# Streamed weights read back from sixteen parts of one DRAM tile instead of from a contiguous copy each

## The chip, the cores and the metric

The kernel runs on one core of a Trainium2 chip. The metric is the device time of one execution in microseconds; lower is better. Times given as a median come from several unprofiled runs; the profile is of one execution with the hardware profiler on. In what follows PE is the matmul engine (PEld its weight loads), DVE the vector engine, ACT the scalar engine, POOL the general-purpose engine and SP the sync engine, which here does nothing but issue transfers. Sixteen DMA engines carry every transfer, whichever engine issues it. SBUF has 128 rows (partitions).

## The reference

The input x is 2048 rows of 1024 numbers in bf16. Each row is first layer-normalised. Two things are then computed from the normalised rows and added to x. Path A is an attention over 64 segments of 32 rows, one after the other, with a memory of 8 rows that the next segment takes from the output of the one before:

```python
for s in range(n_seg):                       # 64 segments, strictly in order
    h = jnp.concatenate([mem, xs], axis=1)   # 8 memory rows + 32 rows of x
    q = jnp.einsum('btd,dhe->bhte', h, Wq)   # 32 heads of 128; Wk, Wv the same
    ...
    p = _softmax(jnp.where(mask, scores * scale, -1e9))
    o = jnp.einsum('bhte,hed->btd', jnp.einsum('bhqk,bhke->bhqe', p, v), Wo)
    mem = o[:, :M, :].copy()
    outs.append(o[:, M:, :])
```

Path B picks the two rows with the highest router score, sends them through a gated feed-forward block (w_gate, w_up, w_down) and adds the result to those rows.

## The kernel before

**Weights.** Wq, Wk, Wv and Wo are 32 MB together, more than SBUF holds. They are cut into 64 granules of 128 x 2048 numbers (512 KB): granules 0 to 47 are eight granules (one for each 128 rows of the model dimension) for each of six phases (q, k and v, each in two halves of the heads), granules 48 to 63 are two heads of Wo each. 44 granules stay in SBUF, three are kept in pieces, and seventeen are read anew in every segment; they are listed in `streamed`. Three of the seventeen (11, 15 and 58) have some of their columns kept on chip, so that 1600, 1536 and 1728 columns of each row travel instead of 2048.

**The copies.** In the inputs a row of such a granule is part of a longer row. In segment 0 each streamed granule is therefore copied, from DRAM to DRAM, into a tile of its own (`wsc[g]`, 128 rows one behind the other). `copy_block` issues the copies on POOL's queue, in three batches of at most six, among the work of segment 0 that prepares the memory rows of all segments (the "left rows"). Segments 1 to 63 read these tiles.

**The stream.** `fetch` takes the next granule of the list `flow`, gets one of five slots (`wstream`, each 128 rows of 4 KB) and issues its load on SP's queue. `after` calls it when PE has been given the last matmul of a streamed granule, so the next load waits for that slot alone. The order is that of the program; nothing is planned at run time. A streamed granule is used by PE in the loop over phases (line 862) or in `project` (line 922). For the whole of segments 1 to 63 SP issues hardly anything else; POOL issues the small transfers of a segment (the rows of x, the prepared values QKL and VL, the outputs).

**Loads from sixteen places.** Rows of x are also addressed as `x_left = x2.rearrange("(t s r) d -> t s r d", t=4, s=16)`. The left rows of a tile t are `x_left[t, :, XM:SEG, :]`: the last 8 rows of 16 segments, that is sixteen places in DRAM, 64 KB apart, with eight consecutive rows of 2 KB each, for 128 rows of SBUF. They are loaded at the start (tile XLR, line 230, two loads on SP's queue and two on ACT's) and once more at the end (tile XLS, line 683, four loads on SP's queue). VL, a small tile of prepared values, is read from sixteen places too (line 619). All other large loads name 128 rows on both sides, but for four loads of w_down at the end (line 503), which reach 64 rows of SBUF each.

Of the kernel before, what the change touches and what calls it, by code (L numbers as in the profile page):

```python
# [8 lines left out]
BF16 = mybir.dt.bfloat16  # L9
# [13 lines left out]
PART, AT_HOME = 58, 320  # L23
# [9 lines left out]
def kernel(  # L33
# [16 lines left out]
    nc = tc.nc  # L50
    P = 128
    Bsz, S, D = A_x.shape
# [28 lines left out]
    streamed = [1, 4, 11, 15, 21, 23, 29, 34, 37, 41, 45, 47, 50, 54, 56, 58, 63]  # L81
# [4 lines left out]
    def granule_dram(g):  # L86
        if g < 48:
            p, kc = divmod(g, KC)
            mat, half = PHASES[p]
            return Wqkv[mat][kc * P:(kc + 1) * P, 2048 * half:2048 * (half + 1)]  # L90
        w = g - 48
        return Wo2[2 * w * P:(2 * w + 2) * P, :].rearrange("(hh e) d -> e hh d", hh=2)
# [11 lines left out]
    def granule_out(t, g):  # L104
        return t[:, :] if g < 48 else t.rearrange("p (hh d) -> p hh d", hh=2)
# [3 lines left out]
    dram = ctx.enter_context(tc.tile_pool(name="dram", bufs=1, space=DRAM))  # L109
# [12 lines left out]
    ol_d = [dram.tile([P, 16, XL * H], BF16, name=f"ol_d{t}") for t in range(4)]  # L122

    at_home = {PART: AT_HOME, LAST_KEPT: LAST_COLS, GUEST: 512}
    wsc = {g: dram.tile([P, 2048 - at_home.get(g, 0)], BF16, name=f"wsc{g}") for g in streamed}
    r_d = dram.tile([1, S], BF16, name="r_d")

    res_tiles = {}
# [4 lines left out]
    def room(g, name):  # L133
        if g not in place:
            return home(g, [P, 2048], BF16, name)[:, :]
        tag, i = place[g]
        return areas[tag][:, i, :]
# [14 lines left out]
    def travelling(g):  # L152
        w = granule_dram(g)
        if g in (LAST_KEPT, GUEST):
            return [(slice(0, 2048 - at_home[g]), w[:, 0:2048 - at_home[g]])]
        if g != PART:
            return [(slice(0, 2048), w)]
        return [(slice(0, D - AT_HOME), w[:, 0, AT_HOME:D]), (slice(D - AT_HOME, 2048 - AT_HOME), w[:, 1, :])]
# [47 lines left out]
    for s in range(4):  # L206
        nc.vector.tensor_copy(out=SELM[:, s, 0:XM, :],
                              in_=IDENT[:, 32 * s:32 * s + XM].unsqueeze(2).to_broadcast([P, XM, 4]))
# [197 lines left out]
    def fetch():  # L406
        if not flow:
            return
        s, g = flow.pop(0)
        t = wstream.tile([P, 2048], BF16, tag="g", name="g")  # L410
        if g == PART and s < NSEG - 1:
            n = 2048 - AT_HOME
            for c, w in travelling(g) if s == 0 else [(slice(0, n), wsc[g][:, :])]:
                nc.sync.dma_start(out=t[:, c], in_=w)
            t = (OP, t)
        elif s == 0 or g == PART:
            nc.sync.dma_start(out=granule_out(t, g), in_=granule_dram(g))
        elif g in (LAST_KEPT, GUEST):
            nc.sync.dma_start(out=t[:, 0:2048 - at_home[g]], in_=wsc[g][:, :])
            if g == GUEST:  # L420
                t = [t[:, 512 * c:512 * (c + 1)] for c in range(3)]
        else:
            nc.sync.dma_start(out=t[:, :], in_=wsc[g][:, :])
        queued.append((g, t))

    def part(t, jq):
# [45 lines left out]

    def copy_block(g):
        for c, w in travelling(g):
            nc.gpsimd.dma_start(out=wsc[g][:, c] if g in at_home else granule_out(wsc[g], g), in_=w)

    to_copy = list(streamed)
    flow += [(s, g) for s in range(NSEG) for g in (streamed if s else first_streamed) if s or g != GUEST]
# [44 lines left out]
    for g in range(KC):  # L523
        if g in first_streamed:
            assert flow.pop(0) == (0, g)
            t = wstream.tile([P, 2048], BF16, tag="g", name="g")
            queued.append((g, t))
        else:
            t = res_tiles[g] = room(g, f"wres{g}")
# [10 lines left out]
    for g in range(KC, 32):  # L540
        if g == GUEST:
            t = res_tiles[g] = room(v_homes[8], "guest")
            nc.sync.dma_start(out=t, in_=granule_dram(g))
        elif g in first_streamed:
            if len(queued) < N_SLOT:
                fetch()
        else:
            load_resident(g)
        if g >= 8 and g < 15:
            load_x(g - 7)  # L550
# [70 lines left out]
    def left_done(p):  # L621
        for g in range(8 * p, 8 * (p + 1)):
            if g in first_streamed and g != GUEST:
                fetch()
        if p == 0:
            sd_rows(MV[:, 1:NT, :], VE[:, 1:NT])
            spread(1, NT)
            router_tiles()
        elif p == 1:
            res_tiles.pop(GUEST)  # L630
            load_resident(v_homes[8])
            area("big0", [P, 8, 2048], "W8A")
            for g in AREAS["big0"]:
                load_resident(g)
        elif p == 2:
            router_top()
            route_rows()
        elif p == 3:
            route_turns(*routed[0])
            load_resident(hx)  # L640
            home_first()
        elif p == 4:
            area("big1", [P, 8, 2048], "W8B")
        elif p == 5:
            load_resident(hm)
        if p in (1, 2):
            copy_blocks(6)

    def copy_blocks(n):
        for _ in range(min(n, len(to_copy))):  # L650
            copy_block(to_copy.pop(0))

    def after(s, g):

        if g in streamed:
            fetch()
        if s == NSEG - 1:
            if g in resident and g < 48 and g not in place and g not in resident[:3]:
                free_homes.append(g)
            if g in (54, 55):  # L660
                for t in (2 * g - 108, 2 * g - 107):
                    load_left_x(t)
            if g >= 57:
                fetch_moe(1)
# [62 lines left out]
    for s in range(NSEG):  # L727
# [120 lines left out]
        for p, (mat, half) in enumerate(PHASES):  # L848
            PSm = psA.tile([P, 512], F32, tag="acc", name="PSm")
            behind = []  # L850
            for kc in range(KC):
                g = 8 * p + kc
# [3 lines left out]
                for jq in range(4):  # L856
                    rhs = [(0, 512, part(Gv, jq))]
                    if s > 0 and g == LAST_KEPT and jq == 3:
                        n = 512 - LAST_COLS
                        rhs = [(0, n, Gv[:, 1536:1536 + n]), (n, 512, back[g][:, 0:LAST_COLS])]  # L860
                    for c0, c1, w in rhs:
                        nc.tensor.matmul(PSm[32 * jq:32 * jq + 32, c0:c1], lhsT=ST[:, kc, :], rhs=w,  # L862
                                         start=(kc == 0), stop=(kc == KC - 1), tile_position=(0, 32 * jq))
# [250 lines left out]
```

## Time and profile before

| | |
|---|---|
| median of 3 runs | 1817.13 us (1808.01 to 1818.28) |
| the profiled execution | 1815.76 us, span of its instructions 1814.0 us |
| PE busy | 1564.0 us, 86% of the span |
| DVE, ACT, POOL busy | 941.3, 781.4, 331.0 us |
| DMA | 657.62 MB, mean 363 GB/s |
| SP's queue (q1) | 601.13 MB, 88.1% of the time of 16 DMA engines |
| mean granted clock of PE | 0.987 |

The span falls into three stages: up to about 230 us the weights come in and segment 0 runs, with the preparation of the left rows; from 230 to 1725 us segments 1 to 63 run, all alike, some 24 us each; then the left rows' outputs and path B follow. A busy time is the sum over an engine's instructions and says nothing about what it waits for; that stands in the views of waits. The DMA share is the time that packets took on the sixteen engines, and can pass 1 by a few hundredths where a packet's record overlaps the next. Instructions that only issue a transfer are not counted as busy; a view of one tile shows how long each took and how long the transfer was under way.

### The profile page before, as it was taken

Reading aid. Unit: us, or ns where it says so; the run is one execution under the profiler, and the core shown is the slowest. Engines: PE = TensorE matmul, PEld = TensorE weight load, DVE = VectorE, ACT = ScalarE, POOL = GpSimd, SP = SyncE. Lnnn points to the kernel's source line nnn. Section 1 sums busy time; section 2 is a strip of 40 time slices with the busy share of each in tenths; the row PEclk is TensorE's granted clock in tenths of the full one; section 3 lists DMA queues with packets and bytes.
Section 4 is the critical chain, followed back from the end, with each engine's and each line's share of the span. In section 5 each row is a group of like instructions: output and inputs, shape, how many; then the busy total and the mean of one; then the engine's idle time right before and its main releaser. Section 6 shows DMA issues by size and latency. Waiting matters only on the chain. (4 is left out here: it accounts for less than half of the span.)

```text
span 1814.0 us, 70576 instructions
## 1 busy us (share of the span) xinstructions
PE 1564.0 (86%) x30354; PEld 851.3 (47%) x30354; DVE 941.3 (52%) x3027; ACT 781.4 (43%) x2032; POOL 331.0 (18%) x610
## 2 busy tenths in 40 slices
PE   8999888888888888888888888888888888888888
PEld 5444444444444444444444444444444444444455
DVE  6722155555555555555555555555555555555531
ACT  2333144444444444444444444444444444444410
POOL 1021311111111111111111111111111111111220
PEclk9999989999999999999999999999999999999989
DMA  9685899999999999999999999999999999999998
GB/s 359 232 297 192 270 357 368 382 369 375 376 392 386 376 377 379 375 374 375 382 373 387 383 384 366 389 393 370 368 382 383 379 382 369 381 376 378 386 375 300
DMA packets 215833, 657.62 MB, mean 363 GB/s; under 512 B 42800, under 2 KB 46432, under 8 KB 215520
## 3 DMA queue, kind: packets, MB, share of 16 engines
q1 hardware_dynamic: 189232, 601.13, 88.1%
q0 software_dynamic: 25264, 50.14, 8.1%
q8 instruction: 237, 3.88, 0.9%
q10 hardware_dynamic: 1024, 1.84, 0.3%
q14 instruction: 76, 0.62, 0.1%
HBM read 632.01 MB, written 29.56 MB: 365 GB/s over the span
## 5 line engine op out<-in xcount | busy, mean ns | idle before, releaser
L862 PE MATMUL PSm<-wres,ST 128*32 128x512 bf16 x6400 | 501.6, 383 | 0.0
L862 PEld LDWEIGHTS <-ST 128*32 128x32 bf16 x12351 | 325.3, 96 | 351.0 <-issue 111.4
L862 PE MATMUL PSm<-g,ST 128*32 128x512 bf16 (+1 forms) x3017 | 307.0, 380 | 55.9 <-DMA g<-wsc 52.5
L922 PEld LDWEIGHTS <-OT 128*32 128x32 bf16 x8255 | 215.6, 97 | 80.1 <-issue 63.3
L450 ACT COPY BK<-KEPT 128x512 bf16<-128x512 bf16 x252 | 152.3, 605 | 131.2 <-PE WO L922 68.1
L871 ACT CAST XB<-PSm 128x512 bf16<-128x512 f32 x256 | 150.3, 587 | 126.3 <-PE PSm L862 124.8
L668 POOL DMA_DIRECT2D QKL<-ql_d x63 | 46.4, 736 | 773.6 <-ACT OTL L821 756.8
L922 PE MATMUL WO<-W8B,OT 128*32 128x256 bf16 x4096 | 185.6, 276 | 0.2 <-issue 0.2
L862 PE MATMUL PSm<-W8A,ST 128*32 128x512 bf16 x2048 | 182.7, 381 | 0.2 <-DVE RXT L346 0.2
L922 PE MATMUL WO<-g,OT 128*32 128x256 bf16 (+1 forms) x2497 | 130.1, 276 | 46.8 <-DMA g<-wsc 38.4
L450 DVE COPY BK<-KEPT 128x512 bf16<-128x512 bf16 x252 | 106.9, 424 | 121.9 <-ACT BK L450 73.6
L955 POOL DMA_DIRECT2D out_dram<-XN x256 | 131.1, 517 | 177.6 <-DVE XN L951 165.3
L862 PE MATMUL PSm<-BK,ST 128*32 128x512 bf16 x693 | 123.3, 386 | 22.5 <-DVE ST L399 22.5
L892 ACT CAST VM<-PSm 128x512 bf16<-128x512 f32 x128 | 79.7, 623 | 98.3 <-PE PSm L862 98.2
L748 DVE COPY KT<-PSm 128x512 bf16<-128x512 bf16 x126 | 51.0, 405 | 124.3 <-PE PSm L738 124.3
L738 PEld LDWEIGHTS <-XB 128*128 128x128 bf16 x1024 | 58.0, 98 | 105.0 <-ACT XB L871 98.7
L765 DVE TENSOR_TENSOR BS<-BS,CT 128x96 f32<-128x96 f32 (+1 forms) x256 | 59.6, 233 | 90.2 <-PE BS L758 85.7
L738 PE MATMUL PSm<-IDENT,XB 128*128 128x128 bf16 x1008 | 100.5, 222 | 2.8
L743 ACT COPY QT<-PSm 128x512 bf16<-128x512 bf16 x126 | 73.8, 586 | 55.7 <-PE PSm L738 55.7
L783 DVE TENSOR_REDUCE DN<-BS 128x8 f32<-128x320 f32 x128 | 62.8, 490 | 64.4 <-ACT BS L775 64.4
L565 PE MATMUL PSG<-XLT,wres 128*128 128x512 bf16 x336 | 94.4, 383 | 1.1 <-ACT GA L567 0.9
L951 DVE CAST XN<-WO 128x256 bf16<-128x256 f32 x64 | 27.2, 424 | 129.0 <-PE WO L922 129.0
(222 smaller groups left out, 2422.6 us busy)
## 6 DMA issues: line engine op xcount, KB each, us to landing
g<-wsc SPq DMA_DIRECT2D x882, 512.0 KB, 6.1
g<-wsc SPq DMA_DIRECT2D x62, 432.0 KB, 5.7
g<-wsc SPq DMA_DIRECT2D x63, 400.0 KB, 6.1
g<-wsc SPq DMA_DIRECT2D x63, 384.0 KB, 6.4
ql_d<-GA POOLq DMA_DIRECT2D x16, 512.0 KB, 6.6
QKL<-ql_d POOLq DMA_DIRECT2D x63, 128.0 KB, 6.1
MW<-in_B_w_gate_dram SPq DMA_DIRECT2D x16, 448.0 KB, 13.7
wres<-in_A_Wk_dram SPq DMA_DIRECT2D x12, 512.0 KB, 10.2
```

Source lines behind the costliest of these rows:

```text
L450: copy(out=back[g][c], in_=KEPT_COLS[g][c])
L565: nc.tensor.matmul(PSG[:, :], lhsT=part(Gs[kc], h // 4)[:, P * (h % 4):P * (h % 4 + 1)], rhs=XLT[:, :, kc, :], start=(kc == 0), stop=(kc = ...
L738: nc.tensor.transpose(out=PTq[:, il, :, :].rearrange("p j r -> p (j r)"), in_=XB[:, il * P:(il + 1) * P], identity=IDENT[:, :])
L743: nc.scalar.copy(out=QT[half][:, :, :], in_=pv)
L748: (nc.vector.tensor_copy if s else nc.scalar.copy)(out=KT[half][:, :, 0:32], in_=pv)
L765: nc.vector.tensor_tensor(out=S4, in0=S4, in1=m, op=ALU.add)
L783: nc.vector.tensor_reduce(out=DN[:, :], in_=S8, axis=AX.X, op=ALU.add)
L862: nc.tensor.matmul(PSm[32 * jq:32 * jq + 32, c0:c1], lhsT=ST[:, kc, :], rhs=w, start=(kc == 0), stop=(kc == KC - 1), tile_position=(0, 32 ...
L871: nc.scalar.copy(out=XB[:, :], in_=PSm[:, :])
L892: nc.scalar.copy(out=VM[half][:, :], in_=PSm[:, :])
L922: nc.tensor.matmul(PS[32 * g:32 * g + 32, c0:c1], lhsT=lhs(h), rhs=rhs, start=False, stop=(last and hs == 1), tile_position=(0, 32 * g), s ...
L955: nc.gpsimd.dma_start(out=out2[s * SEG:s * SEG + XM, 256 * g:256 * (g + 1)], in_=OB[32 * g:32 * g + XM, :])
```

## The change

The seventeen tiles become one, `wsc_d`, of sixteen parts. Part e holds, for each streamed granule in turn, the eight rows 8e to 8e+7 of the granule, one behind the other, and the next granule's eight rows follow directly. `wsc[g]` is now a view of that tile with sixteen parts of eight runs (`e i c`). A whole granule is thus sixteen pieces of 32 KB, and a part is 33,536 x 8 numbers long. Loads and copies use the view in place of a 128-row tile. Copies of the granules of Wo, which were one transfer with both heads, are issued as one transfer per head. Sizes, slots, queues and the order of loads are untouched.

```diff
     at_home = {PART: AT_HOME, LAST_KEPT: LAST_COLS, GUEST: 512}
-    wsc = {g: dram.tile([P, 2048 - at_home.get(g, 0)], BF16, name=f"wsc{g}") for g in streamed}
+    row_of = {g: 2048 - at_home.get(g, 0) for g in streamed}
+    wsc_d = dram.tile([16, sum(row_of.values()) * 8], BF16, name="wsc_d")
+    wsc, start = {}, 0
+    for g, n in row_of.items():
+        wsc[g] = wsc_d[:, start:start + 8 * n].rearrange("e (i c) -> e i c", i=8)
+        start += 8 * n
...
-            for c, w in travelling(g) if s == 0 else [(slice(0, n), wsc[g][:, :])]:
+            for c, w in travelling(g) if s == 0 else [(slice(0, n), wsc[g])]:
                 nc.sync.dma_start(out=t[:, c], in_=w)
...
-            nc.sync.dma_start(out=t[:, 0:2048 - at_home[g]], in_=wsc[g][:, :])
+            nc.sync.dma_start(out=t[:, 0:2048 - at_home[g]], in_=wsc[g])
...
-            nc.sync.dma_start(out=t[:, :], in_=wsc[g][:, :])
+            nc.sync.dma_start(out=t[:, :], in_=wsc[g])
...
     def copy_block(g):
         for c, w in travelling(g):
-            nc.gpsimd.dma_start(out=wsc[g][:, c] if g in at_home else granule_out(wsc[g], g), in_=w)
+            if g < 48 or g == PART:
+                nc.gpsimd.dma_start(out=wsc[g][:, :, c], in_=w)
+            else:
+                for hh in range(2):
+                    nc.gpsimd.dma_start(out=wsc[g][:, :, D * hh:D * (hh + 1)], in_=w[:, hh, :])
```

## The prediction

> **What bounds the kernel now.** I read the page's slices first, then the waits of the matmul engine, then the queue that issues the streamed loads, then stretches of time side by side. The page's DMA row has each slice's busy share of the sixteen DMA engines in tenths:
>
> ```profile
> DMA  9685899999999999999999999999999999999998
> ```
>
> From the sixth slice to the last but one it stands at 9. That is the stage in which segments 1 to 63 run, from 230 to 1725 us. Its row in the view by stretches (length, busy time and count of each engine, granted clock, DMA share, GB/s):
>
> ```profile
> 230.00:1725.00 1495.00, 1275.71 (x28193) 696.30 (x28190) 826.76 (x2757) 702.37 (x1879) 280.00 (x506) 0.99 1.01 378
> ```
>
> The DMA engines are busy all the time, at 378 GB/s, so the stage moves 1495 us x 378 GB/s = 565 MB. PE is busy for 1276 of the 1495 us. The streamed granules are nearly all of these bytes:
>
> ```profile
> g<-wsc SPq DMA_DIRECT2D x882, 512.0 KB, 6.1
> g<-wsc SPq DMA_DIRECT2D x62, 432.0 KB, 5.7
> g<-wsc SPq DMA_DIRECT2D x63, 400.0 KB, 6.1
> g<-wsc SPq DMA_DIRECT2D x63, 384.0 KB, 6.4
> ```
>
> Counts times sizes give 527,760 KB, 540 MB, in 1070 loads: one load per 1495/1070 = 1.40 us, while one takes 6.1 us from issue to landing. So more than four of the five slots are always under way, and any loss of rate goes straight into the time. PE waits for these loads for 52.5 + 38.4 = 91 us in all (total, times, longest):
>
> ```profile
> PE PSm L862 <- DMA g<-wsc: 52.5, 102, 1.9
> PE WO L922 <- DMA g<-wsc: 38.4, 100, 1.1
> ```
>
> The stage is therefore close to balance: a faster DMA could win at most those 91 us, since PE has work for the rest, but a slower DMA has nothing that hides it.
>
> **What the change does to a load.** No byte and no wait on PE is added. What changes is the form of the 1070 loads: 128 rows on both sides before, 128 rows of SBUF against sixteen parts of eight runs in DRAM now. The kernel before has this form already, in three small places: the tiles XLR (start), XLS (end) and VL are loaded from sixteen places of eight rows each. Here is SP's queue around the turn from one segment of the stage to the next, before (wsc_105 to wsc_121 are the copies of the seventeen granules, g a slot of the stream):
>
> ```order
> L414 DMA g<-wsc_120 128x1728
> L423 DMA g<-wsc_121 128x2048
> L423 DMA g<-wsc_105 128x2048
> L423 DMA g<-wsc_106 128x2048
> L419 DMA g<-wsc_107 128x1600
> ```
>
> and the same place now:
>
> ```order
> L428 DMA g<-wsc_d 128x1x2048 x11
> L419 DMA g<-wsc_d 128x1x1728
> L428 DMA g<-wsc_d 128x1x2048 x3
> L424 DMA g<-wsc_d 128x1x1600
> L424 DMA g<-wsc_d 128x1x1536
> ```
>
> To compare, the first rows of SP's queue, which are the same before and now but for their line numbers:
>
> ```order
> L1118 UNCONDITIONAL_BRANCH
> L235 DMA XLR<-in_A_x_dram 128x1x1024 x2
> L528 DMA g<-in_A_Wq_dram 128x1024
> L528 DMA wres_165<-in_A_Wq_dram 128x1024
> L528 DMA g<-in_A_Wq_dram 128x1024
> ```
>
> Nothing moved in the order, and the first loads of segment 1 still wait for their copies; the loads now have XLR's shape (128x1xn against sixteen by eight) instead of that of the weight loads (128xn). So XLR and XLS are the price list, and there are two prices in it.
>
> *The issue.* Instructions of SP's queue (ns: min/median/max):
>
> ```profile
> L423 SPq DMA_DIRECT2D g<-wsc x882: 319/320/1075, 224.4 to 1725.2; - x177
> L230 SPq DMA_DIRECT2D XLR<-in_A_x_dram x2: 573/640/707, 0.9 to 1.7; - x2
> L683 SPq DMA_DIRECT2D XLS<-in_A_x_dram x4: 604/657/1584, 1725.6 to 1728.6; - x4
> L619 SPq DMA_DIRECT2D VL<-vl_d x2: 533/540/547, 171.2 to 202.1; - x2
> ```
>
> An issue grows from 0.320 to between 0.540 and 0.657 us, by at most 0.337 us. Seventeen of them take 11 us of a segment of 1495/63 = 23.7 us, so the queue keeps up; behind the issuing instruction stands only the next streamed load. I cost it at nothing, because four loads under way cover it. Without that cover each of five slots comes round 0.337 us later: 1070 x 0.337 / 5 = 72 us.
>
> *The rate.* These are stretches of the same run:
>
> ```profile
> 4.00:7.00 3.00, 3.00 (x31) 3.00 (x29) 2.44 (x6) 0.06 (x1) 2.04 (x4) 1.00 1.06 264
> 8.00:12.00 4.00, 2.54 (x36) 1.91 (x33) 2.77 (x6) 1.45 (x3) 0.00 (x0) 1.00 1.06 378
> 1735.00:1738.00 3.00, 2.25 (x12) 0.83 (x12) 0.74 (x3) 0.00 (x0) 0.87 (x2) 0.50 1.05 296
> 1738.00:1741.00 3.00, 3.00 (x8) 1.15 (x7) 2.70 (x5) 0.00 (x0) 3.00 (x7) 0.50 1.06 264
> 1741.00:1750.00 9.00, 9.00 (x43) 5.95 (x42) 6.91 (x23) 2.78 (x3) 2.50 (x5) 0.99 1.03 398
> 1791.00:1798.00 7.00, 7.00 (x34) 4.66 (x33) 0.00 (x0) 0.00 (x0) 0.00 (x0) 1.00 1.07 230
> 1799.00:1803.00 4.00, 4.00 (x64) 2.81 (x56) 2.25 (x8) 0.00 (x0) 0.00 (x0) 1.00 1.05 385
> ```
>
> From 4 to 7 us most of the four XLR loads passes, and the rate is 264 GB/s with the DMA engines busy throughout (share 1.06). At 8 to 12 us half granules pass, in pieces of 2 KB like XLR's, and it is 378. From 1735 to 1741 us the four XLS loads pass: 296 and 264 GB/s, and 398 as soon as they are through. The engines are not idle in the slow stretches; each packet simply takes longer. So the form itself, or where it reads, costs about 30% of the rate. The row at 1791 to 1798 us says where the cost may lie. There the four w_down loads pass that reach only 64 of the 128 SBUF rows, from rows of DRAM that follow each other, at 230 GB/s; the w_down loads of 128 rows behind them run at 385 (1799 to 1803 us). So the way in which a load's rows are dealt out over SBUF can halve the rate by itself. I take it that a load with sixteen parts is dealt out in eights, part by part, so that engines meet on the same piece of SBUF. That is an inference from these rows, not something they show.
>
> [...]
>
> *The copies.* On POOL's queue the four output-projection granules that were one copy each are two now, before (in brackets the counters of POOL's earlier transfers that an issue waits for):
>
> ```order
> L475 DMA wsc_117<-in_A_Wo_dram 256x1x1024 [waits DMASW6_49]
> L475 DMA wsc_118<-in_A_Wo_dram 256x1x1024 [waits DMASW7_49]
> L475 DMA wsc_119<-in_A_Wo_dram 256x1x1024 [waits DMASW0_49]
> L475 DMA wsc_120<-in_A_Wo_dram 128x704 [waits DMASW1_49]
> L475 DMA wsc_120<-in_A_Wo_dram 128x1024
> L475 DMA wsc_121<-in_A_Wo_dram 256x1x1024
> ```
>
> and now:
>
> ```order
> L484 DMA wsc_d<-in_A_Wo_dram 16x8x1024 [waits DMASW6_49]
> L484 DMA wsc_d<-in_A_Wo_dram 16x8x1024 [waits DMASW7_49]
> L484 DMA wsc_d<-in_A_Wo_dram 16x8x1024 [waits DMASW0_49]
> L484 DMA wsc_d<-in_A_Wo_dram 16x8x1024 [waits DMASW1_49]
> L484 DMA wsc_d<-in_A_Wo_dram 16x8x1024 x2
> L481 DMA wsc_d<-in_A_Wo_dram 16x8x704 [waits DMASW4_49]
> L481 DMA wsc_d<-in_A_Wo_dram 16x8x1024 [waits DMASW5_49]
> L484 DMA wsc_d<-in_A_Wo_dram 16x8x1024 [waits DMASW6_49]
> L484 DMA wsc_d<-in_A_Wo_dram 16x8x1024 [waits DMASW7_49]
> ```
>
> Ten copies stand where six stood, so four issues are added, ahead of the GATE copy of the left rows' values. The trace has six such copies and what comes behind them (start, length):
>
> ```profile
> L475 POOL DMA_DIRECT2D wsc<-in_A_Wo_dram x6: 695/944/1152, 133.6 to 136.3; - x6
> 163.81 0.19 POOL L598 COPY CT<-VG 128x4 bf16<-128x4 bf16 x1 [26.37 <-DVE PT L781]
> ```
>
> Four more at 0.944 us are 3.8 us, in front of a gap of 26.37 us in which POOL waits for DVE: nothing on the path. Uncovered it would be 3.8 us.
>
> **The sum.** The profiled execution took 1815.76 us with a span of 1814.0; the median of the runs is 1817.13, 0.1% more. Of the span 319 us lie outside the stage and stay. Inside, 565 MB at the mean of the three rows, (264 + 296 + 264)/3 = 275 GB/s, take 2057 us in place of 1495: +562 us. 1815.76 + 562 = 2378 us. PE's 91 us of waiting are swallowed in that, not added. Bounds for the rate of 4 KB runs, which no row shows in this form: on the bad side the 64-row loads, 230 GB/s, 2457 us of stage, +962 us, and with the uncovered issue +72: 2850 us. On the good side I halve the loss of the mildest row, (296 + 378)/2 = 337 GB/s, 1677 us, +182 us: 1998 us. I take the middle because the three rows are of the very form, and longer runs speak both ways: fewer changes of row, but longer meetings.
>
> **Rivals.**
> 1. *The slow rows are DRAM's doing.* XLR and XLS read 16 KB out of every 64 KB of x, a power of two; the new parts lie 33,536 x 16 = 536,576 bytes apart, 512 KB and 12 KB. If that pitch made the 264 GB/s, the new loads keep 378, the issue is covered, and the time is 1816 us. For it: no load from sixteen parts with another pitch is in the trace at length. Against it: the 64-row loads show the same loss without any pitch. [...]
> 2. *Faster: each engine reads one run of 32 KB per granule, and the next granule's run behind it.* If DRAM rewards that and SBUF does not punish it, PE's waits for the loads go, and PE's own work is next: 1816 - 91 = 1725 us. It decides only if packets get faster than now, and 378 GB/s is already within 5% of the best row above (398). XLR's runs of 16 KB, consecutive as well, show no such reward.
> 3. *Only the issue counts.* The rate stays and the cover is thinner than the median of 6.1 us says: up to 1816 + 72 = 1888 us.
>
> **Chances.** The forecast's case 0.85, rival 1 0.09, rival 2 0.03, rival 3 0.03. The range 2000 to 2850 us holds about 95% of the forecast's case, 0.81 in all. A measurement of this kernel tells about 1% (18 us; its three runs spread over 0.6%) from no change. Slower: 0.85 + 0.03 = 0.88. Within 1%: 0.08, nearly all of rival 1. Faster: 0.04.
>
> **What would show it.** In the changed kernel's stage the DMA share stays at 1.0 while GB/s falls to about 275; packets and bytes of the streaming queue stay as they are and their share of the longer span does not fall. Issue to landing of the loads rises from 6.1 to some 8 or 9 us (the same four loads under way at 1.92 us each), and PE's waits for them grow from 91 to about 600 us; SP's issues read 0.54 to 0.66 us. If GB/s stays at 378 and only the issues are longer, rival 1 holds and the inference on SBUF is wrong. If the stage's rate lies above 337, the form hurts little with runs of 4 KB. If PE's granted clock falls towards 0.50, as in the rows from 1735 to 1741 us, the time goes above my range.

## The result and the profile after

The change made the kernel a third slower: 2420.16 us, median of 6 runs (2413.52 to 2439.69), against 1812.92 us for the kernel before on the same chip (1807.26 to 1818.56). The ratio is 1.3385, with a 95% interval of 1.3338 to 1.3433. The profiled execution took 2438.65 us, its span 2437.0 us. One run behind the times below, of the kernel with two column halves, took 3085.42 us at a granted clock of 0.554 where its others had 0.99, and is left out of their median.

The DMA row of the page (busy share of the DMA engines in tenths, by slices) and the row of the streaming queue (packets, MB, share of the time of sixteen engines) of the changed kernel:

```profile
DMA  9759999999999999999999999999999999999998
...
q1 hardware_dynamic: 189232, 601.13, 92.4%
```

The same row of the kernel before:

```profile
q1 hardware_dynamic: 189232, 601.13, 88.1%
```

The engines are as full as before, and the queue has the same packets and bytes. In the view by stretches, the stage of segments 1 to 63 of the changed kernel (length, busy us and count of PE, PEld, DVE, ACT and POOL, granted clock, DMA share, GB/s):

```profile
230.00:2344.00 2114.00, 1528.24 (x28182) 768.67 (x28181) 831.86 (x2758) 714.42 (x1881) 278.50 (x505) 0.85 1.03 267
```

The stage grew from 1495 to 2114 us, by 619. The other 323 us of the span were 319 before. So all but 4 us of the loss lies in the stage, where 378 GB/s became 267, while the DMA share went from 1.01 to 1.03: the engines were busy all the time before and after. The page's DMA issues (KB each, median us from issue to landing), and the first line of SP's issues in the view of the new tile (ns: min/median/max):

```profile
g<-wsc_d SPq DMA_DIRECT2D x882, 512.0 KB, 9.3
g<-wsc_d SPq DMA_DIRECT2D x62, 432.0 KB, 9.3
g<-wsc_d SPq DMA_DIRECT2D x63, 400.0 KB, 9.2
g<-wsc_d SPq DMA_DIRECT2D x63, 384.0 KB, 9.0
```

```profile
L428 SPq DMA_DIRECT2D g<-wsc_d x882: 514/514/887, 222.6 to 2344.3; - x177
```

A load lands after 9.3 us where it took 6.1, and its issue takes 0.514 us where it took 0.320. What PE waits for, in the view of waits (total us, times, longest), and the first row of the chain that ended last (shares of the span by engine), both of the changed kernel:

```profile
PE PSm L871 <- DMA g<-wsc_d: 343.7, 400, 2.7
PE WO L931 <- DMA g<-wsc_d: 182.6, 238, 2.3
```

```profile
DMA 73%; PE 25%; issue 1%; ACT 1%; DVE 0%; POOL 0%; ACTq 0%; DVEq 0%; SPq 0%
```

The chain is DMA for 73% of the span; that of the kernel before could be followed over only a fifth of its span, so the two can't be compared. PE now waits 526 us for streamed granules instead of 91. It was also busy for longer in the stage, 1528 us instead of 1276, with nearly the same count of matmuls in the trace, at a granted clock of 0.85 instead of 0.99. That did not add to the time: the DMA engines had no idle time to give, and 565 MB at 267 GB/s are 2116 us, which is the stage.

### The profile page after: what moved, and what is told of

It reads as the page before. It is cut to its first block, busy times and chain, and to the rows that moved or that the text cites. A ratio compares the mean times of both kernels' runs of the same rounds, so it can differ in the third digit from the quotient of the medians.

```text
span 2437.0 us, 70581 instructions
## 1 busy us (share of the span) xinstructions
PE 1816.9 (75%) x30354; PEld 923.5 (38%) x30354; DVE 946.3 (39%) x3027; ACT 793.4 (33%) x2032; POOL 331.3 (14%) x614
## 4 chain that ended last, share of the span: by engine, by line
DMA 73%; PE 25%; issue 1%; ACT 1%; DVE 0%; POOL 0%; ACTq 0%; DVEq 0%; SPq 0%
DMA g<-wsc_d 71%; PE PSm L871 11%; PE PSG L574 4%; PE WO L931 3%; PE WD L1005 2%; PE PSV L601 2%; PE PSm L747 1%; DMA vl_d<-VG 1%; PE FIRST L263 0%; DMA wres<-in_A_Wq_dram 0%; DMA out_dram<-XLS 0%; DMA XLR<-in_A_x_dram 0%; PE BS L819 0%; PE PSm L385 0%; DMA wres<-in_A_Wo_dram 0%
## 5 line engine op out<-in xcount | busy, mean ns | idle before, releaser
L871 PEld LDWEIGHTS <-ST 128*32 128x32 bf16 x12351 | 345.5, 103 | 769.6 <-issue 588.2
L871 PE MATMUL PSm<-g,ST 128*32 128x512 bf16 (+1 forms) x3017 | 339.1, 422 | 347.5 <-DMA g<-wsc_d 343.7
L871 PE MATMUL PSm<-wres,ST 128*32 128x512 bf16 x6400 | 571.5, 431 | 0.0
L931 PEld LDWEIGHTS <-OT 128*32 128x32 bf16 x8255 | 256.9, 113 | 281.3 <-issue 238.5
L931 PE MATMUL WO<-g,OT 128*32 128x256 bf16 (+1 forms) x2497 | 161.5, 336 | 191.0 <-DMA g<-wsc_d 182.6
L931 PE MATMUL WO<-W8B,OT 128*32 128x256 bf16 x4096 | 227.0, 326 | 0.0
L871 PE MATMUL PSm<-W8A,ST 128*32 128x512 bf16 x2048 | 195.4, 406 | 0.2 <-DVE CT L353 0.2
L871 PE MATMUL PSm<-BK,ST 128*32 128x512 bf16 x693 | 143.9, 469 | 22.5 <-DVE ST L404 22.5
L828 DVE CAST OT<-BT 128x128 bf16<-128x128 f32 x128 | 37.4, 292 | 212.8 <-PE BT L822 200.8
L828 ACT CAST OT<-BS 128x128 bf16<-128x128 f32 x130 | 34.5, 265 | 233.9 <-PE BT L822 221.2
```

Source lines behind the costliest of these rows:

```text
L828: copy(out=OT[half][:, 2 * ph + jl, :, :], in_=ov[:, :, 0:SEG])
L931: nc.tensor.matmul(PS[32 * g:32 * g + 32, c0:c1], lhsT=lhs(h), rhs=rhs, start=False, stop=(last and hs == 1), tile_position=(0, 32 * g), s ...
```

## The experiments

What was to be settled is why a load of the same bytes has a lower rate. The theory of the prediction (A in the expectations) puts it at the writing into SBUF: engines meet there when the rows are dealt out in eights. Its rivals are DRAM (B, the place of the parts; D, the reading of parts as such) and the issue time (C). For each run I give its time, beside it the kernel before on the same chip, and the stretch from 500 to 1300 us, which lies in the stage of every kernel. In that stretch the kernel before reads:

```profile
500.00:1300.00 800.00, 684.13 (x15182) 374.05 (x15181) 445.46 (x1487) 377.11 (x1013) 147.45 (x266) 1.00 1.01 380
```

and the changed kernel:

```profile
500.00:1300.00 800.00, 576.98 (x10844) 291.84 (x10837) 318.33 (x1057) 273.26 (x720) 106.08 (x192) 0.87 1.03 270
```

### Sixteen parts, but in seventeen tiles

```diff
-    wsc_d = dram.tile([16, sum(row_of.values()) * 8], BF16, name="wsc_d")
...
+    wsc = {g: dram.tile([16, 8 * n + 64], BF16, name=f"wsc{g}")[:, 0:8 * n].rearrange("e (i c) -> e i c", i=8)
+           for g, n in row_of.items()}
```

> Each copy in a DRAM tile of its own again, as before, but a pad of 128 B behind each eight rows, so that the load still goes out as sixteen parts of eight rows. Theory A (the loss sits in how a load of sixteen parts is dealt out to the engines and written into SBUF): the loads move 262 to 275 GB/s with the DMA engines busy all the time, and the time is that of the change, 2420 us, within 60. Theory B (the loss sits in DRAM: sixteen parts 536,576 B apart in one tile of 8.6 MB): 1815 us, within 25, since the parts lie 32 KB apart here as they did before.

Measured: 2467.7 us (one run; before 1811.41). The same stretch of this kernel:

```profile
500.00:1300.00 800.00, 566.89 (x10420) 286.50 (x10412) 308.30 (x1024) 264.44 (x699) 101.67 (x184) 0.85 1.03 261
```

The parts lie 32 KB and 128 B apart instead of 536,576 B, each granule in a region of its own, and the rate is as low as in the change (1 GB/s below what theory A allowed, the time within its 60 us). Where the copies lie is not the cause; the form of the load is enough.

### One tile, but 128 rows

```diff
-    wsc = {g: dram.tile([P, 2048 - at_home.get(g, 0)], BF16, name=f"wsc{g}") for g in streamed}
+    wsc_d = dram.tile([P, sum(row_of.values())], BF16, name="wsc_d")
+    wsc, start = {}, 0
+    for g, n in row_of.items():
+        wsc[g] = wsc_d[:, start:start + n]
+        start += n
```

> One DRAM tile for all copies, as in the change, but of 128 rows, each holding that row of all granules side by side (67,072 B from row to row), so a load goes out as 128 rows of one run each. Theory A (dealing of the sixteen parts): the rate of before, 378 GB/s, and 1815 us, within 20. Theory B (DRAM: one tile, runs of a granule scattered over it): the runs are scattered more than in the change, single 4 KB pieces 67 KB apart, so 2300 us or more.

And the same tile with rows 131,072 B apart (`dram.tile([P, 65536], ...)`):

> The one tile of 128 rows again (1799.6 us with 67,072 B from row to row), with 131,072 B from row to row, a power of two. Theory A (only SBUF's side counts): 1800 us, within 15. Rival 1 of the prediction (the slow rows of before were DRAM's doing, through a row pitch of a power of two): the rate falls towards 264 GB/s, 2300 us or more.

Measured: 1799.59 us, ratio to before 0.9929 (0.9896 to 0.9961), and 1800.21 us, 0.9943 (0.9914 to 0.9971). The same stretch, of the first and then of the second kernel:

```profile
500.00:1300.00 800.00, 688.11 (x15277) 376.52 (x15272) 447.29 (x1493) 378.67 (x1017) 149.89 (x272) 1.00 1.01 382
```

```profile
500.00:1300.00 800.00, 691.31 (x15386) 380.96 (x15378) 451.19 (x1505) 381.34 (x1022) 150.25 (x272) 1.00 1.02 385
```

A granule scattered in 4 KB pieces over a tile of 8.6 or 16.8 MB streams at the full rate, with a pitch of a power of two as well. With this and the run above, theory B and rival 1 of the prediction are out. Both layouts are a little faster than the kernel before, by 0.4 to 1.0% and 0.3 to 0.9%: PE's waits for the loads fall from 91 to 75 and 64 us. Why one tile serves a little better was not looked into.

### The issue time alone

Two runs hold the 128 rows and lengthen the issue. The first cuts each load into two halves of the columns:

```diff
-            nc.sync.dma_start(out=t[:, :], in_=wsc[g][:, :])
+            for c in (slice(0, n // 2), slice(n // 2, n)):
+                nc.sync.dma_start(out=t[:, c], in_=wsc[g][:, c])
```

> The kernel before with two loads per granule: all 128 rows, the left half of the columns and then the right half, so runs of 2 KB. SP issues 2 x 0.320 = 0.64 us a granule, more than the 0.514 us of the change. Theory C (issue time is the loss): at least the 72 us that more issuing was costed at when nothing hides it, 1880 us or more. Theory A (which engine writes which rows; all 128 rows are in each load as before): the rate of before and 1815 us, within 20. If two loads for one were what made the 64-row halves slow: 2470 us.

The second keeps one load, whose source has two runs of 2 KB in each of its 128 rows:

```diff
-    wsc = {g: dram.tile([P, 2048 - at_home.get(g, 0)], BF16, name=f"wsc{g}") for g in streamed}
+    wsc = {g: dram.tile([P, n + 64], BF16, name=f"wsc{g}") for g, n in row_of.items()}
...
+        return wsc[g].rearrange("p (c x) -> p c x", c=2)[:, :, 0:h]
...
-            nc.sync.dma_start(out=t[:, :], in_=wsc[g][:, :])
+            nc.sync.dma_start(out=t[:, 0:2048].rearrange('p (c x) -> p c x', c=2), in_=two(g))
```

> One load per granule, the source 128 rows of two runs of 2 KB that lie 128 B apart in DRAM; the outermost count is 128 on both sides, but the source has one dimension more than in the kernel before. Theory A3 (the rows are dealt out well when the outermost count is 128 on both sides): 1815 us, within 25. Theory E (only the plain shape, 128 rows of one run, is dealt out well; any further dimension loses it): 2400 us or more, and SP's issue near 0.5 us instead of 0.32.

Measured: 1850.72 us for the two halves (median of three runs, 1849.14 to 1859.93), ratio 1.0229 (1.0194 to 1.0263), and 1839.93 us for the split rows (one run), with before at 1813.4. SP's issues and the stretch of the second kernel:

```profile
L441 SPq DMA_DIRECT2D g<-wsc x882: 517/518/1477, 223.1 to 1749.9; - x177
```

```profile
500.00:1300.00 800.00, 674.96 (x14862) 365.29 (x14862) 435.26 (x1453) 368.94 (x991) 146.39 (x266) 1.00 1.04 372
```

An issue of 0.518 us, which is that of the change, goes with 372 GB/s and 27 us more, not with 267 and 607 more. Even 0.64 us a granule costs only some 40 us (370 GB/s in the same stretch). Both runs also have pieces of 2 KB instead of 4, so the issue has at most these costs, if nothing else in them got faster. Theory C is out as the main cause; so is theory E, since a further dimension of the source alone does no harm. The first run missed both theories' numbers, theory A's by 16 us and theory C's by 29 us.

### Halves of 64 rows

```diff
-            nc.sync.dma_start(out=t[:, :], in_=wsc[g][:, :])
+            for r in range(2):
+                nc.sync.dma_start(out=t[64 * r:64 * r + 64, :], in_=wsc[g][64 * r:64 * r + 64, :])
```

> The copies and their tiles as before; each load is two loads of 64 rows, the lower and the upper half of SBUF's rows, each row one run. No load has sixteen parts. Theory A1 (engines meet on the same piece of SBUF whenever a load reaches only a part of its rows at a time): slow as the loads of 64 rows of the kernel before were at 264 GB/s, so 2300 to 2550 us. Theory A2 (a source in parts by itself costs, whatever rows are written): no parts, so 1815 to 1890 us. Theory C (issue time on SP): two issues of 0.32 us for one, 0.64 us a granule, which is at most 72 us more where nothing hides it: 1815 to 1890 us.

Measured: 2470.22 us (one run; before 1811.41), and in the same stretch of this kernel:

```profile
500.00:1300.00 800.00, 583.86 (x10478) 270.26 (x10474) 310.79 (x1032) 265.40 (x702) 101.63 (x184) 0.82 1.03 262
```

No part is left here, DRAM is read as in the kernel before, and the loss is that of the change. The two column halves above show that two loads for one are not to blame. So parts are one way to lose the rate, and loads that reach half of SBUF's rows another. That what they share lies on SBUF's side is the nearest guess; the next two runs test it for parts. (The 264 GB/s that the expectation gives to the 64-row loads of before was a slip; their row says 230.)

### Out of SBUF: from DRAM to DRAM

In two runs the streamed loads write five DRAM tiles instead of the slots, first from the 128 rows of before, then from the sixteen parts of the change:

```diff
-            nc.sync.dma_start(out=t[:, :], in_=wsc[g][:, :])
+        nc.sync.dma_start(out=sink[fetched[0] % N_SLOT][:, 0:n], in_=wsc[g][:, :])
...
+        nc.sync.dma_start(out=sink[fetched[0] % N_SLOT][:, 0:n], in_=wsc[g])
```

> The kernel before, with the loads of the copies going not into SBUF but into five DRAM tiles of 128 rows (4224 B from row to row), as 128 rows of one run each. Left out: no granule is loaded into the slots after the first segment, and the products run over what the first segment left there, so PE waits for none of these loads and the time says nothing; what is compared is GB/s where the DMA engines are busy all the time, with the next run. All theories: some rate R for DRAM to DRAM, unknown (300 to 390 GB/s).

> As the run before it, from the copies of the change: sixteen parts of eight rows each, going into the same five DRAM tiles. The same is left out. Theory A (the loss is made where sixteen engines write SBUF out of step): no SBUF is written, so the same rate R as with 128 rows, within 5%. Theory D (reading sixteen parts, or making up their descriptors, is slow in itself): R falls by 29%, as 378 fell to 267 GB/s.

Measured: 2024.04 us and 2058.21 us (one run each; before 1813.4), times that say nothing, as the expectation has it. The stretch of the run from 128 rows, and then of the run from sixteen parts:

```profile
500.00:1300.00 800.00, 679.96 (x14897) 380.84 (x14893) 436.95 (x1459) 372.95 (x995) 146.16 (x265) 0.96 1.00 332
```

```profile
500.00:1300.00 800.00, 674.38 (x14694) 376.41 (x14694) 431.73 (x1441) 366.72 (x980) 142.56 (x258) 0.95 1.00 326
```

With the DMA engines busy all the time (share 1.00), sixteen parts move 326 GB/s and 128 rows 332: 2% less, where it is 29% less into SBUF. Reading parts, and making up their descriptors, is no slower than 326 GB/s, so theory D is out as the main cause, and the loss from there down to 270 is made where SBUF is written. A limit of this pair: with DRAM written even 128 rows reach only 332, so a source that could do no more than that would not show in the rates. The trace's records of single packets narrow it further (4 KB packets of the streaming queue that start in this stretch; no view prints them): the median packet takes 159 ns in both runs, as in the kernel before, and 247 ns in the change.

### Which rows: parts of seven, four and two

The first of these runs takes seven of each part's eight rows into 112 neighbouring rows of SBUF. It should tell whether engines meet because their rows lie exactly eight apart:

```diff
+    def wsc7(g):
+        return wsc[g][:, 0:7, :]
...
-            nc.sync.dma_start(out=t[:, :], in_=wsc[g])
+            nc.sync.dma_start(out=t[0:112, :], in_=wsc7(g))
```

> As the change, but a load takes seven rows of each of the sixteen parts and puts them into 112 neighbouring rows of SBUF, so that the engines write seven rows apart instead of eight. Left out: the last sixteen rows of every streamed granule after the first segment, which keep what the first segment left there; the sums run over them all the same. The five slots are five fixed tiles. A load has 7/8 of the bytes, 494 MB of 565 in the stage. Theory A1 (engines whose rows lie eight apart meet on the same piece of SBUF; seven apart they mostly do not): 330 GB/s or more in the stretches where the DMA engines are busy all the time, the stage 1500 us or less, 1700 to 1830 us in all. Theory A2 (a source in sixteen parts costs, whatever rows are written): 267 GB/s, 494 MB in 1850 us, 2170 us in all, within 60. [...]

Measured: 2186.75 us (one run; before 1811.41):

```profile
500.00:1300.00 800.00, 603.38 (x12219) 314.36 (x12211) 357.27 (x1191) 307.87 (x812) 120.00 (x219) 0.93 1.03 270
```

Theory A1 as I had put it fell: seven apart the rate is the same 270. Theory A2's numbers came, but A2 (a source in sixteen parts costs, whatever is written) doesn't fit the pair above, where parts cost 2%. The run has a weakness: its loads reach 112 rows instead of 128, and no run tells what that alone does. What counts stayed open, since 64-row halves without parts were slow too. So I changed the parts, from sixteen of eight rows to 64 of two, with everything else as in the change:

```diff
-    wsc_d = dram.tile([16, sum(row_of.values()) * 8], BF16, name="wsc_d")
+    wsc_d = dram.tile([64, sum(row_of.values()) * 2], BF16, name="wsc_d")
```

> As the change, but the one DRAM tile has 64 parts, each with the runs of two rows of all granules. Theory A (unless the outermost count is 128 on both sides, an engine is handed neighbouring rows, here eight of them again, and meets other engines in SBUF): 262 to 270 GB/s and 2420 to 2470 us. Theory F (sixteen as a count is what hurts, since it equals the number of engines): back towards 1815 us.

Measured: 1845.17 us (one run; before 1810.59). Theory A's claim that the outermost count must be 128 fell with it; theory F (sixteen as a count) and the size of a part were left. The last run lies between:

```diff
-    wsc_d = dram.tile([16, sum(row_of.values()) * 8], BF16, name="wsc_d")
+    wsc_d = dram.tile([32, sum(row_of.values()) * 4], BF16, name="wsc_d")
```

> As the change, with 32 parts of four rows, between the 16 parts of eight (267 GB/s) and the 64 parts of two (371 GB/s). [...] Theory H (two parts handed to an engine are neighbours, eight rows in a row again; only from 64 on the count is dealt differently): 262 to 270 GB/s and 2420 to 2470 us. [...]

Measured: 1847.36 us (one run; before 1811.77). The stretch with 64 parts of two rows, then with 32 parts of four, and SP's issues of the latter:

```profile
500.00:1300.00 800.00, 676.85 (x14838) 366.75 (x14834) 435.49 (x1452) 369.51 (x990) 144.61 (x264) 0.99 1.00 371
```

```profile
500.00:1300.00 800.00, 681.00 (x14896) 368.32 (x14889) 436.35 (x1456) 370.81 (x993) 147.69 (x268) 0.99 1.00 373
```

```profile
L428 SPq DMA_DIRECT2D g<-wsc_d x882: 512/513/1252, 224.3 to 1755.1; - x177
```

Between 32 parts of four rows and sixteen of seven or eight the rate drops from 373 to 270 GB/s, with an issue of the same 0.51 us for four and eight rows and the same kind of source. Theory H is out: 32 parts go within 2 GB/s of 64. That parts of two and four rows are dealt out so that the engines do not meet in SBUF, and parts of seven and eight so that they do, is my guess: which engine wrote which rows is in none of the traces, so it was not shown. Nor is theory F excluded: every slow run from parts has sixteen of them and every fast one 32 or 64, so the number of parts and their size were never told apart. The bytes of a part don't seem to matter: the parts of four rows are 16 KB long, as those of XLR are, whose eight rows went at 264 GB/s in the three microseconds that the prediction shows.

### Every second granule

```diff
-    for g, n in row_of.items():
+    for k, (g, n) in enumerate(row_of.items()):
+        if k % 2:
+            wsc[g] = dram.tile([P, n], BF16, name=f"wsc{g}")
+            continue
         wsc[g] = wsc_d[:, start:start + 8 * n].rearrange("e (i c) -> e i c", i=8)
```

> Every second streamed granule (9 of 17, 53.6% of the bytes) has its copy in the tile of sixteen parts, the others in tiles of their own as before. If each load pays for its own bytes only: 303 MB at 267 GB/s are 1135 us and 262 MB at 378 GB/s are 693 us, a stage of 1828 us and 2147 us in all, within 40. If a load in sixteen parts puts the engines out of step for the load of 128 rows behind it as well: above that, 2200 to 2420 us. If the plain loads bring the engines back into step: below 2100 us.

Measured: 2664.41 us (one run; before 1810.59), slower than the change itself. The stretch, and the two kinds of loads in it (`wsc_d` in sixteen parts, `wsc` in 128 rows):

```profile
500.00:1300.00 800.00, 565.42 (x9634) 276.25 (x9616) 287.31 (x953) 244.97 (x645) 93.05 (x169) 0.77 1.03 241
```

```profile
g<-wsc_d SPq DMA_DIRECT2D x171, 512.0 KB, 10.3
g<-wsc SPq DMA_DIRECT2D x129, 512.0 KB, 10.4
```

If each load paid for its own bytes alone, the rate would lie between those of the two forms; 241 GB/s is below both. A load of 128 rows, 6.1 us among its like, takes 10.4 us among loads in parts; that alone could be waiting behind them, but the records of single packets show more. In the kernel before, 93% of the streaming queue's 4 KB packets in this stretch took at most 175 ns; here it is 6%, although 46% of the streamed bytes come from 128 rows. So a load loses by what other loads do at the same time. That speaks for engines which meet in SBUF, and against a cost that a load bears by itself. None of the three expectations held (the nearest ended at 2420 us). Why the mixture is worse than parts alone is open.

## Why the prediction was right

The forecast was 2378 us, within 2000 to 2850 and slower at 0.88; the median is 2420.16.

- **The stage.** All of the loss was put into the stage, as bytes over a lower rate. The profiled execution came out 61 us above the sum, of which 57 us are the stage (2114 against 2057) and 4 us the rest of the span. The mis-sized term is the rate: 267 GB/s against 275. It was the mean of three rows, 264, 296 and 264, and two of them were closer. That so short rows came so near to a rate held for 2114 us is in part luck: other loads passed in them too (POOL's queue took 28.7% of the DMA time from 1735 to 1738 us), the microsecond before the first row, with XLR's loads under way, moved 342 GB/s, and the run with every second granule shows that two forms together need not give their mean. That the runs are 4 KB instead of 2 KB hardly moved it: two of the rows gave 264, the stage 267.
- **The cause.** "The form itself, or where it reads" was decided for the form by the parts in tiles of their own, and for SBUF by the pair from DRAM to DRAM. The inference that sixteen parts are dealt out in eights held in so far as sixteen parts of eight rows lose the rate and 32 of four or 64 of two do not; the dealing itself is in no trace. My first refinement of it in the experiments, engines in step eight rows apart, did not hold. That the dealing "can halve the rate" was too strong: the prediction's own rows are 230 against 385, and a whole stage of 64-row loads ran at 262 against 380.
- **The issue.** Forecast 0.54 to 0.66 us, measured 0.514. It was costed at nothing under the cover of four loads, at 72 us without it. The kernel with 32 parts tells about what it can cost: 0.513 us an issue and 1847.36 against 1811.77, so 36 us, or 48 against the one tile of 128 rows (1799.59), part of which may still be the dealing. The zero was somewhat too small for a stream at full rate; in the change nothing of it shows, since the DMA engines are busy all the time.
- **PE.** Waits of about 600 us were forecast, 526 came. PE was busy for longer instead, at a clock of 0.85, which I had named only as a risk at 0.50. As the DMA engines set the pace, neither changed the time.
- **The copies.** They were costed at nothing. The rows of the stage and of the remaining span leave 4 us for all that lies outside the stage, so there was nothing to find. Eight single-head copies now take 0.532 us each, where the six copies of the prediction's row took 0.944 in the median, as this row of the view of the new tile shows:

```profile
L484 POOL DMA_DIRECT2D wsc_d<-in_A_Wo_dram x8: 530/532/547, 133.0 to 137.7; - x8
```

- **The rivals.** Rival 1 (DRAM's pitch, 1816 us) fell: in the stretch from 500 to 1300 us sixteen parts 536,576 B apart or 32 KB and 128 B apart are slow (270 and 261 GB/s), 128 rows 131,072 B apart are fast (385). Rival 2 (longer runs pay, 1725 us) fell: neither 8 nor 16 KB in a row beat 380 GB/s (371 and 373). Rival 3 (only the issue, up to 1888 us) fell for the change, but would do for what is left of it with 32 parts of four rows: 1847 us.
- **What would show it.** The DMA share at 1, the rate near 275, the same packets and bytes at a share that does not fall, 8 or 9 us to landing: all four came, the last a little over with 9.3 us.

## What to carry to other kernels

Where the DMA engines are busy all the time, cost a change of layout by the rate that loads of its new form have somewhere in the same trace, and take the bytes over that rate; PE's waits say only how much a faster stream could win. For a load into all 128 rows of SBUF, a layout in DRAM of sixteen parts, each of eight neighbouring rows, cost 29% of the rate here, and cutting the load into halves of 64 rows 31%; 64 parts of two rows or 32 of four cost about 2%, and rows of one run each nothing. Loads of the bad form slowed down the good ones that were under way with them (10.4 us to landing instead of 6.1), so mixing, half and half here, was worse than either (241 GB/s).

## What was not expected of the hardware

- The step is sharp: 373 GB/s with 32 parts of four rows, 270 with sixteen of seven or eight, with the same queue and order.
- Half of the granules in parts gave 241 GB/s, less than all of them (270).
- An issue on SP took 0.320 us for 128 rows of one run and 0.51 to 0.52 us for the sources with one dimension more (128 rows of two runs, 64 or 32 parts, sixteen of eight rows), whether their rate was good or bad. So the length of the issue told nothing of the rate.
- PE's granted clock was lower where PE waited more for granules: 0.99 in the stage before (91 us of waits in the run, the longest 1.9), 0.85 after (526 us, 2.7), and 0.77 in the stretch of the mixture (620 us in its run, 3.0). Nothing was run to find what sets it.
- One tile of 128 rows, with the granules side by side in a row, was slightly faster than a contiguous tile for each granule: 0.9929 (0.9896 to 0.9961).
